# Logits made for four chunks at once, pairs for two chunks, and two score products moved, in a DeltaNet and expert kernel

## The chip, the cores and the metric

The kernel runs on one core of one Trainium2 chip. The metric is device time in microseconds. Before the change the median of 3 runs is 493.04 us (491.14 to 493.22).

## The reference, cut to what matters

Attention comes first, for 4 batches, 8 heads, 768 steps and a head size of 48. Each head of each batch keeps a 48x48 state:

```
k_n = k / (norm(k) + 1e-6)
for t in range(768):
    y[t]  = q[t] @ state
    v_old = k_n[t] @ state
    state = state + beta[t] * outer(k_n[t], v[t] - v_old)
```

The outputs y of all heads, side by side, are the tokens x: 3072 rows of 384. A gate then sends every token to one of 16 experts: 4 group logits `x @ w_group`, the best group, 4 expert logits `x @ w_expert[g]`, the best expert in it, and a weight that is the product of the two softmax values. The result of a token is that weight times `relu(x @ w1) @ w2` of its expert (384 to 1024 to 384). All is float32.

## The kernel before, in words

**Stages.** The 768 steps are cut into 24 chunks of 32 (`C`, `NCH`); one chunk of all 4 batches fills 128 partitions. Chunks go in groups of four (`RG`). A first stage runs attention and gate chunk by chunk, and a second stage runs the 16 experts. In the listing PE is TensorE, DVE VectorE, ACT ScalarE, POOL GpSimd and SP the engine that issues loads. A float32 matmul of the program appears in the trace as two instructions.

**Order of work.** Within the first stage the order on every engine is the order in which the code is written, and each engine takes its list in that order. The DVE list is partly made by small tasks: `inverse(g)` and `route(r)` are generators that `work(n)` advances by a budget, and `allow(...)` lets a task pass a named point.

**Scores.** `gram(u)` (L242) makes the products k k and k q of chunk u: 32 matmuls (64 instructions in the trace) into one PSUM buffer, copied by ACT into `gt` (L262, for the inverse) and `gq` (L268, for the output). It is called for chunks 0 to 7 in the opening (`first_grams`, the k k part of chunks 0 to 3 first and their k q part last), for chunks 8 and 9 just after, and then for chunk u+10 in period u (`ahead_of`). The opening uses three PSUM places in turn (`homes`); later all of `g_ps`, `t_ps` and `l_ps` share the one buffer with the tag "g".

**Inverse.** `inverse(g)` (L289) turns the scores of four chunks over on DVE (L297), takes roots, solves 32x32 triangular systems by DVE products and sums (L367, L373), and turns the result back (L401, `mt`). ACT spreads it into `mtb` (L412), DVE for a few parts (L410). For group 0 the square root is ACT's, and an Exp behind it (L322) loads the table that the gate needs later. For later groups POOL computes the roots.

**A period.** `advance(u)` (L461) has four steps: the state times k (L471), copied to `f`, and the state times q (L480); `w` = inverse times `f` (L488); the state's sum `s_ps` (L499), copied to `s_bd` by two ACT operations (L505); and the output (L513, or L518 for chunks 14 to 19), copied to `x` by ACT (L522) and stored. `mask(u)` and `scale(u)` (L448, it makes `vh` from `kv`) are DVE work for coming chunks, and `put_values` (L458) copies `vh` into PSUM on ACT. `vh` has two buffers.

**Gate.** `logits(u)` (L533) turns the 128 rows of x by three TensorE transposes (L540), copies them (`xt`, L546), multiplies them with `wr` (384x20) by L441, and copies the 20 logits to `lg` (L552). It belongs to chunk u-1 in period u. `route(r)` works on the logits of four chunks: it is started in the period two behind the group's last chunk, finds expert, rank and weight, and ends in sorting products into PSUM (L706), one per period, which period 22 completes and reads.

**Loads.** `begin(...)` ties a load to a moment: ACT writes one column of the tile (L784), which holds the load on SP until ACT has come there. `con` holds constants in two parts; the second holds the identity. Just before the first period the kernel multiplies constants into the state's PSUM place (L817, two matmuls of 128x384), whose result is overwritten later.

Of the kernel before, what the change touches and what calls it, by code (L numbers as in the profile page):

```python
# [16 lines left out]
C = 32  # L17
# [49 lines left out]
def deltanet_then_moe(  # L67
# [27 lines left out]
    BL, DB = 32, DM // 4  # L95
    assert len(SLOTS) == NE == 16 and not any(n <= TILE or n > T * TILE for n in SLOTS)
# [16 lines left out]
    wr = cp.tile([128, DC, NL], F32, name="wr")  # L113
# [63 lines left out]
    with ExitStack() as first:  # L177
# [14 lines left out]
        ENDING = NCH - 2  # L192
        halved = range(LATE, SMALL * RG)
# [46 lines left out]
        def gram(u, home=None, parts=(0, 1)):  # L240
# [47 lines left out]
        def inverse(g):  # L288
# [243 lines left out]

        def logits(u):  # L533

            r = group_of[u]
            if u == groups[r][0]:
                lg_[r] = sm.tile([128, RG, NL], F32, tag="lg", name=f"lg{r}", bufs=3)
            t_ps = ps.tile([128, DC, 128], F32, tag="g", name=f"t_ps{u}")
# [6 lines left out]
            xt = wk.tile([128, DC, 128], F32, tag="xt", name=f"xt{u}")  # L545
            nc.scalar.activation(xt, t_ps, ACT.Copy)  # L546
            yield
            l_ps = ps.tile([128, NL], F32, tag="g", name=f"l_ps{u}")
            for j in range(DC):
                (in_quarters if u >= ENDING else at_once)(l_ps, xt[:, j], wr[:, j], j == 0,  # L550
                                                          j == DC - 1)
            nc.scalar.activation(lg_[r][:, u - groups[r][0]], l_ps, ACT.Copy)  # L552
# [224 lines left out]
        with tc.manual_schedule(engines={mybir.EngineType.PE, mybir.EngineType.DVE,  # L777
# [28 lines left out]
            ahead = advance(0)  # L806
            next(ahead)
# [8 lines left out]
            for n in (H * D, H * D):  # L816
                nc.tensor.matmul(s_ps[:, 0, 0:n], lhsT=ident, rhs=con[:, cols[1]:cols[1] + n],  # L817
                                 start=True, stop=True, skip_group_check=True)
            second = inverse(1)
# [10 lines left out]
            ahead_of = {u: [u + LEAD] if u + LEAD < NCH else [] for u in range(NCH + 1)}  # L830
            begun, x_in = set(), {}
# [45 lines left out]
            for u in range(NCH + 1):  # L877
# [23 lines left out]
                if not later:  # L901
                    next(turned)
# [24 lines left out]
                for v in ahead_of[u]:  # L927
                    gram(v)
                if ahead_of[u] or later or ending:
# [12 lines left out]
                next(step)  # L942
                if u < NCH - 1:
# [385 lines left out]
```

## Time and profile before

| | |
|---|---|
| median of 3 runs | 493.04 us |
| profiled execution, its own time | 492.32 us |
| its span | 490.6 us |
| PE busy in the span | 447.1 us (91%) |
| DVE busy | 236.1 us (48%) |
| ACT busy | 193.8 us (40%) |
| POOL busy | 188.9 us (39%) |

The profile is of one execution. Busy shares are means over stages that differ, so the windows of the next section but one divide the span. The first stage ends near 218 us. In the timeline a row is one instruction or a series of like ones: start, duration, engine, line, operation, output and input, count, and in brackets the idle time of the engine before it with what ended it; "issue" means that no wait of the profile explains it. The granted clock is the share of TensorE's full speed (2.4 GHz) that was granted, 0.50 being 1.2 GHz.

### The profile page before, as it was taken

To read this page: it belongs to the slowest core of one execution; us is meant where nothing else is said; L and a number is where in the kernel's file an instruction comes from. 1 tells how busy PE (TensorE), PEld (TensorE's weight loads), DVE (VectorE), ACT (ScalarE), POOL (GpSimd) and SP (SyncE) were. 2 spreads that over 40 slices of the span, in tenths; PEclk is the share of its full clock that TensorE was granted. 3 is DMA by queue.
4 is the path that set the end of the run, shared out by engine and by line. 5 is a ranking of instruction groups with operands and counts; after the bars stand their busy time and mean duration, and the time that the engine had idled before them with its cause. 6 is when DMAs were issued, how large, how long until landed. Compare 5 with 4: busy or idle time off the path is not lost. (4 is left out here: it accounts for less than half of the span.)

```text
span 490.6 us, 18139 instructions
## 1 busy us (share of the span) xinstructions
PE 447.1 (91%) x7738; PEld 422.6 (86%) x7738; DVE 236.1 (48%) x866; ACT 193.8 (40%) x415; POOL 188.9 (39%) x328
## 2 busy tenths in 40 slices
PE   3437999999999999999999999999999999999992
PEld 3325888888888888889999999999999999999992
DVE  2998999999999994465201201220122012201210
ACT  3416978798887766641112112111211111111110
POOL 0041210634517132102466355544645465265122
PEclk9999999999999989999999999999999999999998
DMA  5466454454356533106978877967977797878830
GB/s 165 141 193 190 154 168 146 131 173 149 93 165 179 180 106 106 59 22 171 364 227 252 277 255 204 310 181 246 339 260 234 270 330 276 253 221 305 278 112 31
DMA packets 56741, 97.07 MB, mean 198 GB/s; under 512 B 18958, under 2 KB 41417, under 8 KB 56659
## 3 DMA queue, kind: packets, MB, share of 16 engines
q1 hardware_dynamic: 50739, 85.89, 54.7%
q0 software_dynamic: 5920, 10.00, 6.7%
q8 instruction: 62, 1.02, 0.9%
q14 instruction: 20, 0.16, 0.1%
HBM read 81.75 MB, written 14.27 MB: 196 GB/s over the span
## 5 line engine op out<-in xcount | busy, mean ns | idle before, releaser
L1113 PE MATMUL y_ps<-hid,w 128*128 128x224 f32 (+15 forms) x768 | 132.2, 331 | 0.0
L1113 PEld LDWEIGHTS y_ps<-hid,w 128*128 128x128 f32 x768 | 129.0, 190 | 0.3
L1094 PE MATMUL h_ps<-xt,w 128*128 128x232 f32 (+14 forms) x720 | 122.7, 330 | 0.0
L1094 PEld LDWEIGHTS h_ps<-xt,w 128*128 128x128 f32 x720 | 120.1, 190 | 0.3
L1066 POOL DMA_INDIRECT xq<-x_dram,from_q x92 | 87.6, 953 | 37.0 <-issue 24.6
L1097 ACT ACTIVATE hid<-h_ps 128x448 f32<-128x448 f32 (+15 forms) x64 | 32.1, 502 | 100.2 <-PE h_ps L1094 100.2
L1116 DVE COPY yt<-y_ps 128x232 f32<-128x232 f32 (+13 forms) x14 | 5.1, 366 | 135.3 <-PE y_ps L1113 135.3
L1125 POOL DMA_INDIRECT out_dram<-yo,to_i x32 | 34.0, 1064 | 91.3 <-DVE yo L1163 80.3
L1118 ACT ACTIVATE yt<-y_ps 128x224 f32<-128x224 f32 (+15 forms) x34 | 11.5, 337 | 116.6 <-PE y_ps L1113 116.6
L373 DVE TENSOR_TENSOR m<-m,below 128x16 f32<-128x16 f32 (+4 forms) x180 | 53.8, 299 | 0.3
L367 DVE TENSOR_TENSOR below<-m 128x16 f32<-128x16 f32 (+4 forms) x180 | 52.5, 293 | 0.1
L505 ACT ACTIVATE s_bd<-s_ps 48x768 f32<-48x768 f32 x46 | 37.0, 805 | 6.0 <-PE s_ps L499 5.1
L1163 DVE TENSOR_SCALAR yo<-yr,gate 128x384 f32<-128x384 f32 (+14 forms) x28 | 11.1, 415 | 48.5 <-DMA yr<-y_dram 39.8
L257 PE MATMUL g_ps<-kqt 48*32 48x64 f32 (+1 forms) x1216 | 19.4, 236 | 15.3 <-issue 7.9
L257 PEld LDWEIGHTS g_ps<-kqt 48*32 48x32 f32 x1216 | 14.8, 116 | 17.8 <-issue 12.9
L488 PEld LDWEIGHTS w_ps<-f,mtb 64*64 64x64 f32 x736 | 23.7, 137 | 5.6 <-ACT f L475 3.8
L412 ACT ACTIVATE mtb<-mt,con 128x256 f32<-128x256 f32 x39 | 28.2, 747 | 0.0
L488 PE MATMUL w_ps<-f,mtb 64*64 64x48 f32 x736 | 26.6, 222 | 1.5 <-ACT f L475 1.4
L499 PE MATMUL s_ps<-w,kv 32*112 32x96 f32 x736 | 24.5, 267 | 1.2 <-issue 0.5
L499 PEld LDWEIGHTS s_ps<-w,kv 32*112 32x112 f32 x736 | 20.5, 172 | 3.8 <-ACT w L492 0.8
L471 PE MATMUL a_ps<-s_bd,kqt 112*32 112x96 f32 x736 | 21.2, 253 | 2.3 <-ACT s_bd L505 1.3
L592 POOL TENSOR_TENSOR acc<-acc,hots 128x16 f32<-128x16 f32 x16 | 4.2, 261 | 47.1 <-DVE hots L590 46.1
(176 smaller groups left out, 577.2 us busy)
## 6 DMA issues: line engine op xcount, KB each, us to landing
w<-in_w_dram SPq DMA_DIRECT2D x29, 1536.0 KB, 8.8
kv<-in_kv_dram SPq DMA_DIRECT2D x24, 416.0 KB, 3.6
kqt<-in_kq_dram SPq DMA_DIRECT2D x20, 448.0 KB, 4.1
x_dram<-x SPq DMA_DIRECT2D x24, 192.0 KB, 2.3
w<-in_w_dram SPq DMA_DIRECT2D x24, 128.0 KB, 3.9
y_dram<-yq SPq DMA_DIRECT2D x36, 84.0 KB, 9.0
yr<-y_dram SPq DMA_DIRECT2D x14, 192.0 KB, 2.4
kqt<-in_kq_dram SPq DMA_DIRECT2D x8, 224.0 KB, 3.9
```

The lines of the kernel that those rows point to most:

```text
L257: nc.tensor.matmul(g_out[quads[b], hh * NP + j, of], lhsT=kqt[rows, 0, j, quads[b]], rhs=kqt[rows, of, j, quads[b]], start=True, stop=True ...
L367: nc.vector.tensor_tensor(t, column.to_broadcast(like), row.to_broadcast(like), op=ALU.mult)
L373: nc.vector.tensor_tensor(to, to, t, op=ALU.add)
L412: nc.scalar.activation(mtb[:, rows, a], from_, ACT.Copy, scale=by)
L488: nc.tensor.matmul(w_ps[b, h], lhsT=mt[b, uu * H + (h % 2) * NP + h // 2], rhs=f[b, h], start=(h == 0), stop=True, skip_group_check=True)
L499: nc.tensor.matmul(s_at[0:KR, b, j], lhsT=k[quads[b], j, 0:KR], rhs=w[quads[b], 2 * j:2 * j + 2], start=(u == 0 and j == 0), stop=True, sk ...
L505: nc.scalar.activation(s_bd[rows, :, :, hh, :], s_at[rows, :, :, hh * D:(hh + 1) * D], ACT.Copy)
L1066: nc.gpsimd.indirect_dma_start(out=xq[:, g, :], out_offset=None, in_=x_dram[:, :].rearrange("n (q c) -> (n q) c", q=4), in_offset=bass.Ind ...
L1094: nc.tensor.matmul(h_ps[:, k], lhsT=w1[:, j, (f + k) * 128:(f + k + 1) * 128], rhs=xt[:, j, 0:R], start=(j == 0), stop=(j == DC - 1), skip ...
L1097: nc.scalar.activation(hid[:, f:f + 2], h_ps, ACT.Relu)
L1113: nc.tensor.matmul(y_ps, lhsT=w2[:, f, j * 128:(j + 1) * 128], rhs=hid[:, f], start=(f == 0), stop=(f == FC - 1))
L1125: put = nc.gpsimd.indirect_dma_start(out=out[:, :], out_offset=bass.IndirectOffsetOnAxis(ap=to[0:P, i:i + 1], axis=0), in_=yo[0:P, :], in_ ...
```

## The change

It has five parts. Nothing else of the program differs.

1. **Pairs for chunks 0 and 1.** The first two score products are made with 64-column weights (two batches together): 16 matmuls instead of 32. ACT copies the even half with a parity factor, and one DVE operation adds the odd half. The Exp that loads the table moves from behind the square root to behind the last score product of the opening.
2. **Scores of chunks 8 and 9** move from ahead of w into period 0; chunks 10 and 11 are both made in period 1. The second one of a period comes behind the output product. The loads that hung on them are begun behind the first spread of inverse 0.
3. **Constants ahead of w.** The matmuls of constants are seven instead of two.
4. **Logits of chunks 0 to 15.** In period u the three transposes of chunk u-1 go into one tile for four chunks (for u below 14 at the end of the period). In periods 5, 9, 13 and 17 `logits_of` makes the logits of four chunks: `wr`, padded to 32 columns, is the weight, the tokens of a chunk are the moving operand, and each chunk has one strip of 32 columns of the array. The result is copied, turned back together with the next chunk's transposes, and copied to `lg`. Chunks 16 to 23 keep their own logits.
5. **Routes** of the first four groups start one period later.

```diff
@@ gram @@
+            if paired:
+                for j in range(NP):
+                    for b in pairs:
+                        for hh in range(2):
+                            k = kqt[hh * 64:hh * 64 + D, 0, j, b]
+                            nc.tensor.matmul(g_out[b, hh * NP + j], lhsT=k, rhs=k, start=True,
+                                             stop=True, skip_group_check=True)
+                even, odd = cut["parity"][:, 0:1], cut["parity"][:, 1:2]
+                part = wk.tile([128, H, C], F32, tag="part", name=f"part{u}")
+                nc.scalar.activation(part, g_out[:, :, 0], ACT.Copy, scale=even)
+                nc.vector.scalar_tensor_tensor(
+                    gts[g][:, :, uu].rearrange("p t h -> p h t"), in0=g_out[:, :, 1], scalar=odd,
+                    in1=part, op0=ALU.mult, op1=ALU.add)
+                return
@@ inverse @@
-                nc.scalar.activation(rooted, cut["tiny"], ACT.Exp)
@@ logits @@
+        def turn_x(u):
+            g, uu = divmod(u, RG)
+            if uu == 0:
+                xts_of[g] = wk.tile([128, RG, DC, 128], F32, tag="xt", name=f"xt{g}", bufs=1)
+            n = DC + len(turned_logits)
+            t_ps = ps.tile([128, n, 128], F32, tag="g", name=f"t_ps{u}")
+            for j in range(DC):
+                nc.tensor.transpose(out=t_ps[:, j], in_=xs[u][:, j * 128:(j + 1) * 128],
+                                    identity=ident)
+            if turned_logits:
+                logits_by_token(t_ps[:, DC])
...
+            nc.scalar.activation(xts_of[g][:, uu], t_ps[:, 0:DC], ACT.Copy)
+        def logits_by_token(t_ps=None):
...
+            nc.tensor.transpose(out=t_ps, in_=l_sb, identity=ident)
+            lg_[r] = sm.tile([128, RG, NL], F32, tag="lg", name=f"lg{r}", bufs=3)
+            nc.scalar.activation(lg_[r], t_ps.rearrange("p (u e) -> p u e", e=BL)[:, :, 0:NL],
+                                 ACT.Copy)
+        def logits_of(r):
+            l_ps = ps.tile([128, 128], F32, tag="g", name=f"l_ps{r}")
+            for j in range(DC):
+                for uu in range(RG):
+                    nc.tensor.matmul(l_ps[quads[uu]], lhsT=wr[:, j], rhs=xts_of[r][:, uu, j],
+                                     start=(j == 0), stop=(j == DC - 1), skip_group_check=True)
+            l_sb = wk.tile([128, 128], F32, tag="l_sb", name=f"l_sb{r}", bufs=1)
+            nc.scalar.activation(l_sb, l_ps, ACT.Copy)
@@ opening @@
-                gram(u, homes[i % len(homes)], parts)
+                gram(u, homes[i % len(homes)], parts, i < 2)
...
+            nc.scalar.activation(rooted, cut["tiny"], ACT.Exp)
...
-            for u in range(2 * RG, LEAD):
-                gram(u, homes[u % len(homes)])
-                begin(after_gram[u])
...
-            for n in (H * D, H * D):
+            for n in [H * D] * 7:
...
                 allow(ACT_STEP)
+            for u in range(2 * RG, LEAD):
+                begin(after_gram[u])
@@ periods @@
+            ahead_of.update({u: [2 * RG + 2 * u, 2 * RG + 2 * u + 1] for u in range(2)})
...
-                r = group_of.get(u - 2)
-                if r is not None and group_of.get(u - 1) != r and r < NGR - 2:
+                r = group_of.get(u - 3)
+                if r is not None and group_of.get(u - 2) != r and r < NGR - 2:
                     start(route(r), 0.25)
+                if 1 < u < LOGITS + 2 and u % RG == 1:
+                    logits_of((u - 2) // RG)
...
-                for v in ahead_of[u]:
+                for v in ahead_of[u][:1]:
                     gram(v)
...
                 next(step)
+                for v in ahead_of[u][1:]:
+                    gram(v)
+                if early:
+                    next(turned)
```

Here `LOGITS` is 16 and `early` is u below 14.

## Rows read from the trace of the kernel before

**Rows 1.** Busy time by stage: the stretch in us, its length, busy us of each engine with its instructions, granted clock, DMA share, GB/s.

```profile
43.00:146.00 103.00, 96.57 (x3259) 85.29 (x3254) 101.83 (x424) 86.69 (x171) 33.77 (x102) 1.00 0.48 147
146.00:188.00 42.00, 39.13 (x1240) 34.83 (x1238) 39.58 (x152) 30.66 (x62) 19.65 (x51) 0.96 0.52 157
188.00:218.00 30.00, 29.23 (x698) 26.28 (x694) 13.88 (x68) 17.89 (x40) 2.15 (x2) 1.00 0.18 56
218.00:484.00 266.00, 263.67 (x1634) 262.03 (x1632) 49.55 (x104) 44.54 (x101) 125.17 (x141) 1.00 0.77 248
```

**Rows 2.** What DVE waited for between 10 and 180 us: us in total, times, longest.

```profile
DVE m L297 <- ACT gt L262: 8.0, 1, 8.0
DVE vh L448 <- PE w_ps L488: 1.9, 1, 1.9
```

**Rows 3.** Timelines of DVE, ACT and PE around the hand-over of the inverses of chunks 16 and 20.

```profile
152.25 1.18 DVE L401 STREAM_TRANSPOSE mt<-m 128x1024 f32<-128x1024 f32 x1
...
178.56 1.25 DVE L401 STREAM_TRANSPOSE mt<-m 128x1024 f32<-128x1024 f32 x1
...
157.31 1.43 ACT L412 ACTIVATE mtb<-mt,con 128x256 f32<-128x256 f32 x2
...
159.17 1.13 PE L488 MATMUL w_ps<-f,mtb 64*64 64x48 f32 x32 [0.65 <-ACT f L475]
...
187.51 1.14 PE L488 MATMUL w_ps<-f,mtb 64*64 64x48 f32 x32
```

**Rows 4.** Timeline of all engines, the opening.

```profile
6.84 0.53 PE L257 MATMUL g_ps<-kqt 48*32 48x32 f32 x31
...
9.22 0.49 PE L257 MATMUL g_ps<-kqt 48*32 48x32 f32 x33 [1.84 <-issue]
9.82 0.60 ACT L262 ACTIVATE gt<-g_ps 128x256 f32<-128x256 f32 x1 [2.13 <-PE g_ps L257]
10.45 1.25 DVE L297 STREAM_TRANSPOSE m<-gt 128x1024 f32<-128x1024 f32 x1 [7.96 <-ACT gt L262]
...
12.10 1.28 ACT L322 ACT_TABLE_LOAD   x1
```

**Rows 5.** Timeline of all engines from the second part of the constants to the second group's turn (the last row from the DVE timeline further on).

```profile
30.74 0.22 POOL L803 COPY what<-con 128x48 f32<-128x48 f32 x1 [15.30 <-DMA con<-in_const_dram]
...
34.12 0.66 PE L257 MATMUL begin<-kqt 48*32 48x32 f32 x37 [5.27 <-issue]
...
35.73 1.25 DVE L401 STREAM_TRANSPOSE mt<-m 128x1024 f32<-128x1024 f32 x1
...
37.88 0.38 SPq L203 DMA_DIRECT2D kv<-in_kv_dram  x1
...
38.34 0.88 PE L257 MATMUL g_ps<-kqt 48*32 48x64 f32 x38 [1.52 <-issue]
...
39.16 2.93 PE L817 MATMUL s_ps<-con 128*128 128x384 f32 x4
...
42.01 1.17 PE L488 MATMUL w_ps<-vh,mtb 64*64 64x48 f32 x32
...
43.23 0.56 DVE L448 TENSOR_TENSOR vh<-kv,normt 128x384 f32<-128x384 f32 x1 [1.86 <-PE w_ps L488]
...
55.94 1.24 DVE L297 STREAM_TRANSPOSE m<-gt 128x1024 f32<-128x1024 f32 x1
```

**Rows 6.** Timeline of PE from w(2) to w(3), one period with a gram.

```profile
56.82 1.13 PE L488 MATMUL w_ps<-f,mtb 64*64 64x48 f32 x32
57.88 0.86 PE L257 MATMUL g_ps<-kqt 48*32 48x64 f32 x64
58.67 1.04 PE L499 MATMUL s_ps<-w,kv 32*112 32x96 f32 x32
59.84 0.84 PE L441 MATMUL l_ps<-wr,xt 128*128 128x20 f32 x6
60.62 1.13 PE L513 MATMUL o_ps<-w,gqm 64*64 64x48 f32 x32
61.68 0.87 PE L471 MATMUL a_ps<-s_bd,kqt 112*32 112x96 f32 x32
...
63.14 0.55 PE L540 MATMUL t_ps<-con,x 128*128 128x128 f32 x3
63.62 1.14 PE L488 MATMUL w_ps<-f,mtb 64*64 64x48 f32 x32
```

**Rows 7.** The page's list of loads: count, KB each, median us from issue to landing.

```profile
kv<-in_kv_dram SPq DMA_DIRECT2D x24, 416.0 KB, 3.6
```

**Rows 8.** Timeline of PE, the state products that open periods 15, 16 and 19.

```profile
150.82 0.87 PE L471 MATMUL a_ps<-s_bd,kqt 112*32 112x96 f32 x32
...
156.88 0.90 PE L471 MATMUL a_ps<-s_bd,kqt 112*32 112x96 f32 x29 [0.15 <-ACT s_bd L505]
...
178.42 1.34 PE L471 MATMUL a_ps<-s_bd,kqt 112*32 112x96 f32 x32
```

**Rows 9.** PE by the microsecond around the half clock: stretch, length, busy, granted clock, DMA share, GB/s.

```profile
179.00:180.00 1.00, 1.00 (x33) 0.50 0.56 200
```

**Rows 10.** What PE waited for between 42 and 216 us: us in total, times, longest.

```profile
PE g_ps L257 <- issue: 2.5, 4, 0.8
```

More of the change, by code (lines that the diff above doesn't have):

```diff
@@ L95, in deltanet_then_moe @@
     BL, DB = 32, DM // 4
+    assert NL <= BL
     assert len(SLOTS) == NE == 16 and not any(n <= TILE or n > T * TILE for n in SLOTS)
@@ L112, in deltanet_then_moe @@
     ident, before, ones = cut["ident"], cut["before"], cut["ones"]
-    wr = cp.tile([128, DC, NL], F32, name="wr")
+    wr = cp.tile([128, DC, BL], F32, name="wr")
     acc = cp.tile([128, NCH + 1, NE], F32, name="acc")
@@ L192, in deltanet_then_moe @@
         ENDING = NCH - 2
+        LOGITS = NCH - 2 * RG
         halved = range(LATE, SMALL * RG)
@@ L238, in deltanet_then_moe, with gram @@
         begun_with = {}
-        def gram(u, home=None, parts=(0, 1)):
+        def gram(u, home=None, parts=(0, 1), paired=False):
             g, uu = divmod(u, RG)
@@ L531, in deltanet_then_moe @@
         sorted_in = {}
[L533 to L538, printed above, removed]
+        xts_of, turned_logits = {}, {}
+        def turn_x(u):
[4 more added lines that the diff above has]
+            t_ps = ps.tile([128, n, 128], F32, tag="g", name=f"t_ps{u}")
             for j in range(DC):
@@ L544, in logits @@
             xs.pop(u)
-            xt = wk.tile([128, DC, 128], F32, tag="xt", name=f"xt{u}")
-            nc.scalar.activation(xt, t_ps, ACT.Copy)
-            yield
[L548 to L552, printed above, removed]
+            nc.scalar.activation(xts_of[g][:, uu], t_ps[:, 0:DC], ACT.Copy)
+        def logits_by_token(t_ps=None):
+            (r, l_sb), = turned_logits.items()
+            turned_logits.clear()
+            if t_ps is None:
+                t_ps = ps.tile([128, 128], F32, tag="g", name=f"lt_ps{r}")
+            nc.tensor.transpose(out=t_ps, in_=l_sb, identity=ident)
[10 more added lines that the diff above has]
+            nc.scalar.activation(l_sb, l_ps, ACT.Copy)
+            turned_logits[r] = l_sb
+        def logits(u):
+            r = group_of[u]
+            if u >= LOGITS and u == groups[r][0]:
+                lg_[r] = sm.tile([128, RG, NL], F32, tag="lg", name=f"lg{r}", bufs=3)
+            turn_x(u)
+            yield
+            if u >= LOGITS:
+                xt = xts_of[u // RG][:, u % RG]
+                l_ps = ps.tile([128, NL], F32, tag="g", name=f"l_ps{u}")
+                for j in range(DC):
+                    (in_quarters if u >= ENDING else at_once)(l_ps, xt[:, j], wr[:, j, 0:NL], j == 0,
+                                                              j == DC - 1)
+                nc.scalar.activation(lg_[r][:, u - groups[r][0]], l_ps, ACT.Copy)
             yield
@@ L805, in deltanet_then_moe @@
                                   .to_broadcast([128, 4, 4, BL]))
-            ahead = advance(0)
-            next(ahead)
-            for u in range(2 * RG, LEAD):
-                gram(u, homes[u % len(homes)])
-                begin(after_gram[u])
             begin_with.close()
@@ L815, in deltanet_then_moe @@
             sorted_in.update(at=s_ps[:, 0, H * D:H * D + T * 3 * NE], begun=True)
-            for n in (H * D, H * D):
+            for n in [H * D] * 7:
                 nc.tensor.matmul(s_ps[:, 0, 0:n], lhsT=ident, rhs=con[:, cols[1]:cols[1] + n],
                                  start=True, stop=True, skip_group_check=True)
+            ahead = advance(0)
+            next(ahead)
             second = inverse(1)
@@ L900, in deltanet_then_moe @@
                 later, ending = LATE <= u < NCH - 2, u + 2 == NCH
-                if not later:
+                early = u < LATE
+                if not later and not early:
                     next(turned)
@@ L926, in deltanet_then_moe @@
                     gathered = gather_first(found_0)
-                for v in ahead_of[u]:
+                for v in ahead_of[u][:1]:
                     gram(v)
-                if ahead_of[u] or later or ending:
+                if early:
+                    next(step)
+                elif ahead_of[u] or later or ending:
                     next(step)
@@ L942, in deltanet_then_moe @@
                 next(step)
+                for v in ahead_of[u][1:]:
+                    gram(v)
+                if early:
+                    next(turned)
                 if u < NCH - 1:
@@ L1311 @@
         beta=bt.reshape(128, NCH // RG * C), const=const,
-        wr=wr.reshape(DM // 128, 128, G + G * Eg).transpose(1, 0, 2),
+        wr=np.pad(wr, [(0, 0), (0, 32 - wr.shape[1])]).reshape(DM // 128, 128, 32).transpose(1, 0, 2),
         w1=w1.reshape(G * Eg, 4, DM // 128, 32, F).transpose(0, 2, 1, 3, 4).reshape(G * Eg, DM, F),
```

## The prediction

> **What bounds the kernel now.** I read the stages first [rows 1]: from 43 to 146 us PE is busy 96.57 of 103 us and DVE 101.83, ACT only 86.69; from 188 on DVE has slack; from 218 to 484 PE is busy 263.67 of 266. So the expert stage is a PE-bound block that only moves with the end of the first stage, and the change touches the first stage alone. There two engines are full, and the reader has to see which one sets the pace. By its waits DVE waits only twice for more than half a microsecond between 10 and 180 us, 8.0 us at its start and 1.9 us once [rows 2]: it works through its fixed list at its own speed. PE does too. Who is ahead is told by the hand-over every four chunks (w(u) is the first TensorE product with the inverse of chunk u, L488): for chunk 16 DVE ends the inverse at 152.25 + 1.18 = 153.43, ACT takes it at 157.31, w(16) starts at 159.17; for chunk 20 DVE ends at 179.81 and w(20) starts at 187.51 [rows 3]. So now PE, with ACT between its steps, sets the time, and DVE comes next with 157.31 - 153.43 = 3.9 us in hand at chunk 16. What PE saves beyond those 3.9 us plus what DVE itself gains is not paid out.
>
> **The start of DVE's list.** Its first transpose runs at 10.45, behind ACT's copy of chunk 3's scores at 9.82, behind matmuls that stop after 31 of 64 and go on at 9.22 with a hole of 1.84 that no wait explains [rows 4]. Such holes come after matmul 223, 350, 477, 604, 731 and 858 of the program, 127 apart (the first is the 64 + 128 + 31 of [rows 4], the last stands before the 38.34 row [rows 5]; six in all): the instruction stream arrives in blocks. Pairs for chunks 0 and 1 take 2 x 32 matmuls out, so chunk 3 ends at matmul 192, inside the block. Its matmuls then end near 7.5 instead of 9.7 (they start about 0.3 earlier, and 33 of them take 0.49), the copy of 0.60 near 8.3. Lead 2.1 us; bounds 0 (something else of chunk 3 is late) and 2.3. The two added DVE operations (128x256) cost 0.2 to 0.6 us each, below the vh row of 0.56 for 128x384 [rows 5], inside the 7.96 us in which DVE idles: nothing. The page Runtime: NRT & Kernel Launch of the Trainium skill (Instruction fetch mechanics) says that crossing a block boundary is mostly hidden. The holes of 1.84 and 5.27 us [rows 4, 5] say otherwise here; by the page this term would be nothing, and 486.6 below would be 488.7.
>
> **Where w(0) starts.** Now at 42.01, behind two fillers (39.16, 2.93 us for 4 instructions), behind the scores of chunks 8 and 9, behind two holes of 5.27 and 1.52 us [rows 5]. After: 704 matmuls of scores instead of 896 stand before the fillers, so matmul 731 falls inside w(0) and the hole of 5.27 no longer stands in front. The fillers read constants that land at 30.74 (the POOL row) or, since the earlier bursts of loads shift by about a microsecond, near 29.5. Fourteen instructions follow: at the 0.7 us that four now take on average, 9.8 us; if they run at twice the speed from about the middle on, 7.4. End between 36 and 39.3; I take 36.9. The inverse is ready at 35.73 + 1.25 - 2.1 and one spread of 0.7, so 35.6: PE is last here. Lead of w(0): 5.1 us, bounds 2.7 and 6. The table load (1.28 us [rows 4]) that moves behind the scores lies where ACT waited for PE in the hole of 5.27; without that cover it costs 1.5 us, still under the fillers.
>
> **Periods 0 and 1.** Each gets one more gram, 0.80 us by the distance of 57.88 to 58.67 [rows 6]. In period 1 the turn of x now stands behind the second gram in the one shared PSUM buffer and waits for two ACT copies (0.60 for the first [rows 4]), about 1.0 us. The first logits (0.78, 59.84 to 60.62) go. w(0) to w(2), 14.8 us before [rows 5, 6], becomes 16.5. Lead of PE at w(2): 3.4, bounds 1.0 and 4.3. DVE wants the copy of chunk 11's scores at 55.94 [rows 5] less its lead; it comes near 50.6: no stall, and 1 us of one if w(0) comes 3 us later.
>
> **DVE's second lead.** Its wait of 1.86 at 43.23 is for w(0) [rows 5] and goes. Next late is that operation's own data: the load of kv 2 was issued at 37.88 and now stands on SP behind a load that ACT releases only after the first spread, about 36.2; kv loads land 3.6 us after issue in the median [rows 7], so near 40.6 with another load ahead. DVE's lead becomes 43.23 - 40.6 = 2.6 us; bounds 1.5 and 4.0 (2.1 + 1.9).
>
> **Periods 2 to 13.** Per chunk, six matmuls of 128x128 by 20 columns go (0.78 us). Per four chunks come 24 of 128x32 by 128 columns and one transpose. The trace has no such form. Nearest is L471, 112x32 by 96 columns: 32 instructions are busy for 0.87 us [rows 6], 0.027 each, times 128/96: 24 take 0.87. Upper end: the four column strips don't overlap, 24 x 0.13 as for L441's six: 3.1. I take 0.87, for L471 works on the same strips. The transpose is 0.16 (63.14 to 63.62 for three). So (4 x 0.78 - 0.87 - 0.16) / 4 = 0.5 us a period, at the upper end -0.04. A period without a gram takes 6.06 (150.82 to 156.88 [rows 8]), held by the round through ACT, and the gram's matmuls stand where PE waits for ACT in that round, so against 6.80 (56.82 to 63.62 [rows 6]) there is room for the 0.5. Twelve periods give 6.0 us; PE alone would lead by 9.4 at w(14). The page TensorEngine Tiling (Array Packing) of the Trainium skill (Tiling Modes, Key Properties) says that tiles work in parallel, but that a change of the tiling mode drains the array. L471's 0.027 us agrees with the parallel part; the new group follows matmuls of the same strip form, so by the page it drains once behind itself, which no row here prices.
>
> **Where it is capped.** At w(16) DVE allows 2.6 + 3.9 = 6.5 us. PE's 9.4 is above it, so PE waits some 3 us for DVE around chunks 12 to 16 and 6.5 are left. Between 14 and 19 the round of 6.06 holds, so nothing is saved; period 17 pays for its 24 logit matmuls ahead of w, 0.6. The routes start a period later, so one more sorting pair is left over in period 22, 0.2. At w(20) DVE allows 2.6 + 187.51 - 179.81, over 10, and doesn't bind. Sum: 6.5 - 0.6 - 0.2 = 5.7 us off the profiled execution's 492.32 (span 490.6 and 1.7 around it): 486.6; off the median of 493.04, 0.7 above that execution: 487.3. I say 487.0.
>
> **The rivals.** (1) More: DVE keeps the full lead of 4.0, and the stretch at half clock (0.50 at 179 us [rows 9]) isn't met again before the tail: 4.0 + 3.9 - 0.8 + 1.0, about 8, 484.5. For it: both of DVE's waits have named causes that go; against: kv 2. Chance 0.13. (2) Less: DVE's lead is at its lower bound (1.5 + 3.9 - 0.8 = 4.6), or the strips don't overlap and PE keeps the lead of w(2) alone (3.4 - 0.5 - 0.8 = 2.1): 488 to 490.5, say 489. For it: the missing form; against: L471. Chance 0.19. (3) No change: the instruction stream is the pace. A faster PE uses up its blocks faster, and what it saves comes back as holes, as the 5.27 and 1.52 now do; w(0) leads by 2.7, w(2) by 1.0, and the 0.8 at the end eats it: 492.5. For it: matmul 731 now lies inside w(0); against: 2.5 us of such holes ahead of grams in all from 42 to 216 [rows 10]. Chance 0.10. (4) Slower: the clock. PE, now the engine that waits, falls to half speed again and again; about 179 to 182 one such stretch made a state product 1.34 us [rows 8] instead of 0.87, and three groups of that size together lose about 1.5. From period 14 on a round has no slack, so four such stretches there or in the tail outweigh 5.7 us, and seven give 492.5 + 5 = 497. For it: PE will idle in about a tenth of each period; against: a granted clock of 1.00 from 43 to 146 and 0.96 to 188, one fall in all [rows 1]. Chance 0.08.
>
> **How the numbers follow.** Forecast 0.50 (484.8 to 488.8), rivals as above. About 0.5%, 2.5 us, is what can be told from no change: 490.6 and 495.5 are the lines. Faster: 0.50 + 0.13 + most of rival 2 (0.15) = 0.78; same 0.04 + 0.09 = 0.13; slower 0.09. The range leaves out the better half of rival 1, rival 4 and most of rival 3: 483.8 to 491.2.
>
> **What would show it.** Right: the first DVE transpose near 8.3; fillers from about 29.5 and w(0) near 37; no DVE wait above 1 us behind it; 24 strip matmuls in under 1 us; ACT's spreads for chunk 16 waiting for DVE, and w(20) near 181.6. Wrong: w(0) after 40, a DVE wait above 2 us for the scores of chunk 11 or for kv 2, logit groups of 2 to 3 us, or a granted clock of 0.50 in several stretches after 45 us.

## The result, and the profile after

The changed kernel takes 497.38 us in the median (493.56 to 500.26, 20 runs), the kernel before 493.13 (489.06 to 503.41, 20 runs). The ratio, which leaves out executions more than 1.5% above the fastest of their kernel, is 1.0097, with a 95% interval of 1.0072 to 1.0122: slower by 1%, where 487.0 and "faster" had been forecast. The profiled execution took 499.14 us (span 496.9; before 492.32 and 490.6).

By stage, the columns being those of [rows 1], with the borders behind 146 moved to the changed kernel's times:

```profile
43.00:146.00 103.00, 91.10 (x3151) 79.56 (x3128) 98.17 (x407) 80.53 (x156) 34.74 (x95) 0.92 0.46 143
146.00:192.00 46.00, 40.37 (x1380) 35.77 (x1380) 43.30 (x168) 35.25 (x70) 19.33 (x53) 1.00 0.50 156
192.00:226.00 34.00, 32.60 (x731) 28.96 (x724) 15.35 (x72) 17.43 (x40) 5.75 (x7) 0.90 0.16 49
226.00:490.00 264.00, 262.07 (x1566) 260.68 (x1565) 48.30 (x99) 43.86 (x99) 125.17 (x140) 1.00 0.78 250
```

The expert stage is what it was: 262 of 264 us of PE. The first stage now runs at a granted clock of 0.92 and 0.90 in two of its three stretches. PE alone, in finer stretches (length, busy, granted clock, DMA share, GB/s):

```profile
38.00:44.00 6.00, 5.00 (x244) 1.00 0.88 253
44.00:48.00 4.00, 0.71 (x31) 1.00 0.81 227
49.00:61.00 12.00, 11.10 (x288) 0.50 0.30 96
62.00:95.00 33.00, 29.26 (x1093) 1.00 0.52 155
96.00:99.00 3.00, 3.00 (x63) 0.50 0.21 71
100.00:208.00 108.00, 98.79 (x3303) 1.00 0.44 137
209.00:215.00 6.00, 6.00 (x110) 0.50 0.34 93
```

Three stretches at the lower level (1.2 GHz) instead of the one of [rows 9], and ahead of the first one PE does almost nothing for four microseconds. The opening, from the timeline of all engines (to be compared with [rows 4, 5]):

```profile
7.75 0.88 PE L273 MATMUL g_ps<-kqt 48*32 48x32 f32 x64
...
9.30 1.25 DVE L313 STREAM_TRANSPOSE m<-gt 128x1024 f32<-128x1024 f32 x1 [1.35 <-ACT gt L278]
...
31.23 6.33 PE L863 MATMUL s_ps<-con 128*128 128x384 f32 x14 [2.17 <-DMA con<-in_const_dram]
...
37.66 1.14 PE L503 MATMUL w_ps<-vh,mtb 64*64 64x48 f32 x32
...
38.13 0.38 SPq L205 DMA_DIRECT2D kv<-in_kv_dram  x1
38.60 0.85 SPq L201 DMA_DIRECT2D kqt<-in_kq_dram  x2
...
42.02 0.79 PE L528 MATMUL o_ps<-w,gqm 64*64 64x48 f32 x21 [1.00 <-issue]
...
44.72 0.56 DVE L463 TENSOR_TENSOR vh<-kv,normt 128x384 f32<-128x384 f32 x1 [3.28 <-DMA kv<-in_kv_dram]
...
48.87 1.18 PE L495 MATMUL o_ps<-s_bd,kqt 112*32 112x96 f32 x21 [4.16 <-issue]
```

w(0) starts at 37.66, 4.35 us earlier than before, as forecast. Then DVE waits 3.28 us for kv 2, and PE stops in the middle of a group of 32 (11 before, 21 after) for 4.16 us with no wait that the profile shows. The DMA view of those microseconds, 40.5 to 46 and 46 to 47, tells what is missing (packets, MB, share of 16 engines):

```profile
q1 hardware_dynamic: 480, 1.60, 102.3%
...
q1 hardware_dynamic: 145, 0.25, 84.5%
q8 instruction: 1, 0.02, 7.1%
```

For 5.5 us the queues carry loads and not one packet of instructions; the one that comes after 46 is followed by PE at 48.87. How long a packet can take to come is told by two blocks: the kernel before began one at 34.12 [rows 5], and the next packet ran before 36, with load packets at 15% and less; the changed kernel began one at 42.02, and the next packet ran after 46, with load packets at 86% and more. Later the trace has nine such packets in the 40 us from 60 to 100. How far the changed kernel is behind (w(u) after minus before, us; the last row is the changed kernel's second profile, from run e17_again):

| | w(0) | w(1) | w(2) | w(3) | w(13) | w(18) | w(22) | w(23) | span |
|---|---|---|---|---|---|---|---|---|---|
| profile | -4.35 | +0.26 | +5.19 | +4.56 | +4.02 | +3.82 | +2.24 | +6.04 | +6.3 |
| second profile | -3.33 | -0.82 | +4.32 | +7.19 | +4.24 | +3.58 | +1.58 | +2.74 | +3.6 |

The loss is made between w(0) and w(2), 24.35 us where 14.81 were before, and partly won back; the end differs from one execution to the next.

### The profile page after: what moved, and what is told of

The parts are those of the page before. It is cut to its first block, busy times and chain, and to the rows that moved or that the text cites. A ratio compares the mean times of both kernels' runs of the same rounds, so it can differ in the third digit from the quotient of the medians.

```text
span 496.9 us, 18024 instructions
## 1 busy us (share of the span) xinstructions
PE 448.8 (90%) x7688; PEld 422.6 (85%) x7688; DVE 237.9 (48%) x868; ACT 193.1 (39%) x407; POOL 193.4 (39%) x328
## 4 chain that ended last, share of the span: by engine, by line
PE 61%; issue 12%; DMA 9%; ACT 9%; POOL 4%; SPq 1%; DVE 1%; POOLq 0%; DVEq 0%
PE y_ps L1173 19%; PE h_ps L1154 19%; PE w_ps L503 4%; PE s_ps L514 3%; DMA y_dram<-yq 3%; PE a_ps L486 3%; DMA kqt<-in_kq_dram 3%; ACT s_bd L520 3%; PE o_ps L495 3%; DMA yr<-y_dram 2%; PE o_ps L528 2%; PE g_ps L273 2%; ACT mtb L427 2%; POOL out_dram L1185 1%; PE t_ps L558 1%
## 5 line engine op out<-in xcount | busy, mean ns | idle before, releaser
L388 DVE TENSOR_TENSOR m<-m,below 128x16 f32<-128x16 f32 (+4 forms) x180 | 51.9, 288 | 0.4
L1223 DVE TENSOR_SCALAR yo<-yr,gate 128x384 f32<-128x384 f32 (+14 forms) x28 | 11.2, 415 | 44.6 <-DMA yr<-y_dram 36.9
L318 POOL MEMSET m<- 128x256 f32 (+4 forms) x30 | 4.2, 191 | 59.1 <-DVE m L313 59.1
L514 PE MATMUL s_ps<-w,kv 32*112 32x96 f32 x736 | 25.6, 273 | 1.4 <-issue 1.1
L528 PE MATMUL o_ps<-w,gqm 64*64 64x48 f32 x576 | 23.0, 230 | 3.9 <-issue 3.8
L495 PE MATMUL o_ps<-s_bd,kqt 112*32 112x96 f32 x736 | 22.3, 264 | 4.2 <-issue 4.2
L528 PEld LDWEIGHTS o_ps<-w,gqm 64*64 64x64 f32 x576 | 20.3, 144 | 5.9 <-issue 4.3
```

The lines of the kernel that those rows point to most:

```text
L388: nc.vector.tensor_tensor(to, to, t, op=ALU.add)
L495: nc.tensor.matmul(o_ps[quads[b], 2 * j:2 * j + 2, :], lhsT=kqt[0:KR, 1, j, quads[b]], rhs=s_bd[0:KR, b, j], start=(j == 0), stop=False, s ...
L514: nc.tensor.matmul(s_at[0:KR, b, j], lhsT=k[quads[b], j, 0:KR], rhs=w[quads[b], 2 * j:2 * j + 2], start=(u == 0 and j == 0), stop=True, sk ...
L528: nc.tensor.matmul(o_ps[b, h], lhsT=gq[b, hq].rearrange("p a t -> p (a t)"), rhs=w[b, h], start=(u == 0 and h == 0), stop=True, skip_group ...
```

## The experiments

Ratios are to the kernel before on the same chip, with 95% intervals. "Theory 1" is that the four loads begun together behind the first spread hold up kv 2 and PE's instructions.

**The opening alone, and its loads moved.** The opening (e5_head) is the diff without `turn_x`, `logits_of`, `logits_by_token` and without the later start of the routes. The loads (e1_loads) are the whole change with

```diff
             nc.scalar.activation(rooted, cut["tiny"], ACT.Exp)
+            for u in range(2 * RG, LEAD):
+                begin(after_gram[u])
             allow(BEGUN)
...
-            for u in range(2 * RG, LEAD):
-                begin(after_gram[u])
             mask(0)
```

> The kernel before with the opening of the change alone: paired grams of chunks 0 and 1, the Exp behind the grams, scores of chunks 8 to 11 in periods 0 and 1, seven fillers, the loads behind the first spread. Logits and routing stay as in the kernel before. Theory 1 (the four loads hold back kv 2 and the next block of TensorE's instructions): a hole of 3 to 5 us in period 0 or 1, half clock behind it, w(2) at 60 to 62 us and nothing won back later, time 495 to 498 us. Rival (the opening's loss in the changed kernel came from the new logits): w(2) at or before 54 us, time 489 to 491 us.

> The four loads behind the first spread (kqt 10, kv 2, kqt 11 and 12) are begun ahead of the fillers instead, right behind the moved Exp; nothing else changes. Theory 1 (the burst of loads holds back kv 2 and a block of TensorE's instructions, TensorE stands still for 4.16 us in period 1 and its clock halves): no hole of over 2 us in periods 0 and 1, VectorE waits under 1 us for kv 2, the clock is full at w(2), w(2) at about 56 us instead of 62.01, time 488 to 492 us. Rival 1 (TensorE outruns its instructions wherever the loads are): the hole of about 4 us stays, the clock halves behind it, time 496 to 499 us.

Measured: 1.0084 (1.0053 to 1.0114) and 1.0010 (0.9978 to 1.0042). PE with the opening alone, its timeline and then its stretches:

```profile
42.39 0.49 PE L493 MATMUL o_ps<-s_bd,kqt 112*32 112x96 f32 x11
47.31 0.87 PE L493 MATMUL o_ps<-s_bd,kqt 112*32 112x96 f32 x21 [4.43 <-issue]
...
61.52 1.13 PE L501 MATMUL w_ps<-f,mtb 64*64 64x48 f32 x32
```

```profile
44.00:47.00 3.00, 0.00 (x0) 1.00 0.55 170
48.00:61.00 13.00, 13.00 (x303) 0.50 0.28 88
```

The old logits and the same hole at the same place, the same 13 us at half clock, w(2) at 61.52: the opening makes the loss by itself. With the loads earlier (w(0) at 36.99):

```profile
39.81 0.54 PE L528 MATMUL o_ps<-w,gqm 64*64 64x48 f32 x11
43.93 1.31 PE L528 MATMUL o_ps<-w,gqm 64*64 64x48 f32 x21 [3.58 <-issue]
...
57.30 1.14 PE L503 MATMUL w_ps<-f,mtb 64*64 64x48 f32 x32
```

DVE's wait for kv 2 is gone (that `vh` runs at 40.38, unwaited), the half clock behind the hole lasts some 7 us instead of 13.65, and w(2) is at 57.30: 4.7 us come from where the loads stand, and the ratio, 1.0010 against 1.0097, is no longer apart from 1. A second half clock, from 138 to 149, follows a wait of 1.96 us for POOL, of which more below. But the hole stays, 3.58 us, one block earlier; theory 1 as I had put it said that it would go. The packet of instructions again comes only after 41, with load packets at 91% of the queues from 37.5 to 41.

**Loads spread.** Does the hole follow the loads? e9_stagger is e1_loads with kqt 11 and 12 begun only behind the first store of x (its edit, shortened, follows); e19_spread and e20_spread2 were to spread the loads further, on top of mends told below:

```diff
-        after_gram = {2 * RG: [of_kq(2 * RG + 2), (kv_[2], [lambda: load_kv(2)])],
-                      2 * RG + 1: [of_kq(2 * RG + 3), of_kq(NB)]}
+        after_gram = {2 * RG: [(kv_[2], [lambda: load_kv(2)]), of_kq(2 * RG + 2)],
+                      2 * RG + 1: []}
...
+                if u == 0:
+                    load_kq(2 * RG + 3)
+                    load_kq(NB)
```

> The run with the early loads once more, with kv 2 and kqt 10 ahead of the fillers, and kqt 11 and 12 begun only at the end of period 0, so that about 0.9 MB less stands in the queues when period 0 needs its next block of instructions. Theory 1 in its narrower form (the block of instructions stands behind bulk loads in the DMA queues): its packet runs by about 39 us instead of 41.5, the hole in period 0 falls from 3.58 to under 1.5 us, no half clock before 60 us, w(2) at 53 to 55 us instead of 57.30. Rival 1 (a block takes its 6 us from request to use whatever the loads do): the hole stays over 3 us. Time 488 to 491 us by the first, 491 to 493 us by the rival.

> The same spread loads in the version with all four groups' logits at once (sorting of groups 0 to 2 a period later, of group 3 a period earlier than the change has it). The same expectations for periods 0 to 2; ratio 0.985 to 0.994 if the spread takes the hole away, 0.995 to 1.001 if it doesn't.

Measured: 1.0028 (0.9986 to 1.0069) for e9_stagger, 0.9998 (0.9965 to 1.0031) for e20_spread2, 1.0051 (1.0011 to 1.0090) for e19_spread, whose expectation was the same one with a range of 0.985 to 0.995. In e20_spread2 the two loads of kqt 11 and 12 still went out together, at 44.86. PE there, then its stretches:

```profile
44.71 1.31 PE L495 MATMUL o_ps<-s_bd,kqt 112*32 112x96 f32 x32
46.90 1.13 PE L503 MATMUL w_ps<-f,mtb 64*64 64x48 f32 x32 [0.87 <-ACT f L490]
...
50.81 1.30 PE L514 MATMUL s_ps<-w,kv 32*112 32x96 f32 x22 [1.44 <-issue]
...
59.56 1.89 PE L503 MATMUL w_ps<-f,mtb 64*64 64x48 f32 x32
```

```profile
52.00:61.00 9.00, 8.10 (x193) 0.50 0.38 124
```

No hole in period 0, where the queues are empty from 40 to 42; and one in period 1, after 402 load packets and no packet of instructions from 43 to 47.6. In e9_stagger the larger hole likewise moved, from 40.35 to 47.66 (3.20 us; 1.42 were left at 43.14). So the long holes stand where loads run beside the next block. That they would vanish without loads is not shown: no run had an opening without a burst somewhere, and the hole of 1.52 us in the kernel before [rows 5] came with the queues empty from 36 to 37.9. That TensorE outruns its instructions, the rival, is thus true as well, for holes of this size; the loads make them longer. And the clock fell for 9 us behind a wait of 0.87 and a hole of 1.44, so a hole made smaller won nothing here.

**Paired grams and Exp alone** (e12_pairs).

> The kernel before with the paired grams of chunks 0 and 1 and the Exp behind the grams alone. The profile of the changed kernel had the first transpose 1.15 us earlier by them. If that lead reaches the end of the opening: w(0) at about 41 us, ratio 0.997 to 0.999. Rival (the lead is lost in the wait for the constants, for kv 0 and for instructions, as mt(0) of the changed kernel came only 0.18 us earlier): w(0) within 0.3 us of 42.01, ratio 0.999 to 1.002.

Measured 1.0018 (0.9974 to 1.0062): no difference in time. Inside, its profile (of an execution of 498.55 us; the median is 495.83) shows neither of the two expected cases:

```profile
38.04 1.33 PE L501 MATMUL w_ps<-vh,mtb 64*64 64x48 f32 x32
...
43.64 0.55 PE L526 MATMUL o_ps<-w,gqm 64*64 64x48 f32 x12 [1.80 <-issue]
```

w(0) is 3.97 us earlier by the pairs alone, with the scores of chunks 8 and 9 still ahead of it; then come a hole of 1.80 us, half clock from 45 to 58, and w(2) at 58.17, later than before. So in this execution an early w(0) was followed by a hole and a half clock even without the seven matmuls of constants and with the scores and loads in their old order.

**The routing a period later.** e4_logits is the kernel before with the new logits and their routing; e11_late has the old logits and only

```diff
-                r = group_of.get(u - 2)
-                if r is not None and group_of.get(u - 1) != r and r < NGR - 2:
+                r = group_of.get(u - 3)
+                if r is not None and group_of.get(u - 2) != r and r < NGR - 2:
```

> The kernel before with the logits of four chunks at once and the routing of them alone (the opening, the seven fillers and the scores of chunks 8 and 9 stay as before). Theory 1 (the opening loses 5 us, the logits gain): w(2) within 0.5 us of 56.82, each of periods 2 to 13 shorter by 0.3 to 0.5 us, time 489 to 492 us with the tail's loss in it. Rival (the logits themselves are given back to the clock or to the instruction stream): time 493 to 496 us.

> The kernel before with one thing changed: the routing of groups 0 to 3 is started one period later. Logits, opening and everything else stay. Theory 4 (this delay alone puts GpSimd's table behind the place of its use in TensorE's order): a wait of 1 to 4 us for GpSimd in one of periods 8 to 13, half clock behind it, and 14 sorting matmuls in period 22 with w(23) 2 to 4 us later against w(22); time 1.007 to 1.015 of the kernel before. Rival (the delay hurts only because the new logits make TensorE's period shorter than VectorE's and GpSimd's part of it): no wait of over 0.5 us, ratio 0.997 to 1.004.

Measured: 1.0076 (1.0040 to 1.0112) and 1.0064 (1.0024 to 1.0103). In e4_logits w(2) is at 55.15, and PE later waits 4.08 us for POOL, with 10 us of half clock behind it. e11_late, PE, then POOL, then DVE, then PE by stretches:

```profile
105.84 0.55 PE L540 MATMUL t_ps<-con,x 128*128 128x128 f32 x3
109.11 0.46 PE L706 MATMUL s_ps<-mine,at 128*128 128x96 f32 x2 [2.72 <-POOL at L624]
...
99.77 0.21 POOL L640 TENSOR_TENSOR cw<-sums,cw 128x4 f32<-128x4 f32 x1
104.30 3.05 POOL L678 TENSOR_TENSOR what<-what,half 128x24 f32<-128x24 f32 x1 [4.32 <-DVE what L674]
...
103.11 0.20 DVE L664 TENSOR_REDUCE place<-rk 128x4 f32<-128x64 f32 x1
```

```profile
43.00:111.00 68.00, 61.62 (x2140) 1.00 0.46 150
112.00:121.00 9.00, 9.00 (x149) 0.50 0.29 91
122.00:226.00 104.00, 97.56 (x2919) 1.00 0.36 114
```

A period later, DVE has the products of the next inverse in its list ahead of `place`: POOL's `cw` is done by 99.98 and waits 4.32 us for DVE. POOL's product of 24 elements a row then takes 3.05 us; in the kernel before the same one took 0.23, at 98.06. PE's order hasn't moved its first sorting matmul to match, so PE stands 2.72 us, and its clock is at half for some 10 us. The Trainium skill's page SBUF — State Buffer (Terms) says that DVE and POOL share one pair of ports, and that the one that comes second waits for the other's whole instruction; one such wait would be 0.54 us at most here, the longest DVE instruction beside it, so it doesn't explain the 3.05 us by itself. In the kernel before DVE was at work as well, and no run here settles what held POOL.

Two ways out: allow the sorting of groups 0 to 2 a period later (e7_sort: one more `yield NEXT` ahead of the first SORT), or start the routes at the end of the period that turns the logits back (e8_start).

> The logits part alone (as in the run of that part), with the sorting matmuls of groups 0 to 2 allowed one period later, so that TensorE doesn't stand before them for GpSimd's table. Theory 4 (the routing begun a period later puts GpSimd's table behind the place that TensorE's order gives its use; TensorE waits up to 4.08 us there, and its clock halves for 10 us): no wait for GpSimd in periods 8 to 20, no half clock between 100 and 125 us, w(10) at 111 to 113 us instead of 120.17, time 490 to 492 us, and an end no better than before. Rival (the clock falls in those periods because TensorE has less to do): a half clock of like length at another place in periods 4 to 14, time 494 to 497 us.

> The logits part alone, with the routing of a group started at the end of the period in which its logits are turned back (half a period earlier than the change has it, half a period later than the kernel before). Theory 4: GpSimd's first table is ready before TensorE's order comes to it, or the wait is under 1 us; no half clock behind it; the sorting of period 22 falls back to about 12 matmuls as before, time 488 to 491 us. Rival (it isn't the start of the routing): a wait of over 2 us for GpSimd or a half clock of 7 to 10 us stays, time 494 to 497 us.

Measured: 0.9984 (0.9942 to 1.0026) and 1.0126 (1.0079 to 1.0173). With the later sorting, what PE waited for from 42 to 216 us has no wait for POOL over 0.9:

```profile
PE a_ps L487 <- ACT s_bd L521: 4.1, 12, 0.7
...
PE s_ps L457 <- POOL acc L643: 0.9, 1, 0.9
```

and w(10) is at 113.94 (115.57 before). Starting earlier also brought the sorting forward; PE then waited 3.17 us for the same table, until 99.95, and the clock was at half from 101 to 110. What counts here is the order between PE's place for the sorting and DVE's and POOL's list, not the date of the start.

**The end of the pipeline.** In the first profile period 22 holds 14 sorting matmuls (12 before), a half clock follows, and w(23) comes 11.53 us behind w(22) (7.73 before). e2_route and e18_route2, the same kernel twice, give group 3 its old logits and start; e17_again is the changed kernel unchanged:

```diff
-        LOGITS = NCH - 2 * RG
+        LOGITS = NCH - 3 * RG
```

> Chunks 12 to 15 make their logits alone again, and the routing of their group starts in the period in which the kernel before starts it; groups 0 to 2 stay as in the changed kernel. Theory 3 (the late routing puts 14 sorting steps and a wait for GpSimd into period 22, and the clock falls behind it): no half clock between periods 20 and 23, w(23) some 3 to 4 us earlier against w(22) than in the changed kernel, time about 493.5 us. Rival (the clock falls there anyway, or the tail is hidden): time within 1 us of the changed kernel's, 496.5 to 498.5 us.

> The changed kernel once more, unchanged, on the chip of the runs beside it. If the loss belongs to the kernel and not to the chip that it ran on: ratio 1.006 to 1.013, a hole of 3 us and more in period 0 or 1 with half clock behind it, 14 sorting matmuls in period 22. Otherwise (a single chip's or execution's accident): ratio under 1.004.

> The changed kernel with group 3 as in the kernel before, once more, beside the changed kernel on one chip. If the 14 sorting matmuls of period 22 cost what the trace shows (w(23) 3.8 us later against w(22)): ratio 0.006 to 0.008 under that of the changed kernel beside it. If its first run was right (1.020) and the edit itself loses: 0.005 to 0.012 over it. If the two only differ by the clock's chance: within 0.004.

Measured: 1.0200 (1.0151 to 1.0249), then side by side on one chip 1.0097 (1.0059 to 1.0135) for the changed kernel and 1.0117 (1.0069 to 1.0165) for this one. (Why the first of the two measurements of one kernel lies 0.8% above the second isn't known.) That the changed kernel is about 1% slower came out again.

Mending the tail won no time, but the traces of all runs show that there is a loss in it. Between w(22) and w(23), the kernel before, then the changed kernel's second profile:

```profile
201.73 1.58 PE L706 MATMUL s_ps<-mine,at 128*128 128x96 f32 x12
...
203.31 1.13 PE L756 MATMUL s_ps<-mine,at 128*128 128x96 f32 x8
205.15 0.91 PE L756 MATMUL s_ps<-mine,at 128*128 128x96 f32 x6 [0.70 <-POOL at L674]
```

The ten traces with 12 sorting matmuls have w(23) 7.73 us behind w(22), or 9.15 where PE had another wait; of the ten with 14, all with the wait of 0.70 for POOL, six have 8.89 or 10.31, 1.16 more. e11_late, which starts the routes later and does nothing else, is one of the six. In the other four (11.53 to 11.99 us, the changed kernel's first profile among them) the clock was at half there too; in none of the ten with 12. So 1.16 us belong to the 14 matmuls that the later start brings, and 2.6 to 3.1 more to the clock in some executions.

Why did e18_route2 not gain the 1.16? Its edit adds a wait of its own. It puts the turn and the logits of chunk 12 right behind each other at the end of period 13, and PE waits there for ACT's copy:

```profile
147.27 0.27 PE L573 MATMUL t_ps<-con,l_sb 128*128 128x128 f32 x1
148.25 0.84 PE L456 MATMUL l_ps<-wr,xt 128*128 128x20 f32 x6 [0.71 <-ACT xt L565]
```

With this wait and the old logits of four chunks, w(13) to w(22) takes 61.61 us where e17_again takes 59.37: 2.24 lost for 1.16 won. In e2_route half clock from 148 to 155 followed the same wait. The test is thus no evidence against theory 3.

**All mends together.** e10_shift: the logits part alone with the later sorting and group 3's a period earlier. e14_all: the whole change with that and the early loads. e15_tail: the early loads, sorting of groups 0 and 1 later, group 3 as before. e16_noopen: e15_tail without the change's opening.

> The logits part alone with the sorting of groups 0 to 2 one period later (as in the run of that) and the sorting of group 3 one period earlier than the change has it, so that period 22 isn't left with 14 sorting matmuls. Theory 4: no wait of over 1 us for GpSimd, at most about 12 sorting matmuls in period 22, w(23) under 9 us behind w(22), ratio 0.991 to 0.996 of the kernel before. Rival (what the logits save comes back as half clock elsewhere): ratio 0.997 to 1.003 with 6 us or more of half clock between 40 and 220 us.

> The whole change with the loads ahead of the fillers and the shifted sorting of the two runs before. If the losses are the burst of loads and the place of the sorting: the hole in period 0 stays at 2 to 4 us with 3 to 7 us of half clock (as in the run with the early loads), no wait of over 1 us for GpSimd, ratio 0.992 to 0.998 of the kernel before. If the logits' gain is given back to the clock whatever the order: ratio 0.999 to 1.005.

> The whole change, mended in three places: the loads ahead of the fillers, the sorting of groups 0 and 1 one period later, and group 3 (chunks 12 to 15) with logits and routing as in the kernel before. If the three places are where the change lost its time: no wait of over 1 us for GpSimd, about 12 sorting matmuls in period 22, w(23) 7 to 8 us behind w(22), ratio 0.986 to 0.994 of the kernel before. If what is saved comes back as half clock elsewhere: w(22) earlier than 198 us and yet a ratio of 0.997 or more in the mean of the runs, or new stretches of half clock of 6 us and more.

> The same without the change's opening (grams, Exp, fillers and loads as in the kernel before), so logits of chunks 0 to 11 for four at once, sorting of groups 0 and 1 a period later, group 3 as before. Logits alone are worth what w(18) in the run with the shifted sorting showed, 2 to 4 us, if nothing is lost at the end: ratio 0.992 to 0.996. Rival (given back to the clock): 0.998 to 1.003.

Measured: 1.0022 (0.9986 to 1.0057), 0.9967 (0.9929 to 1.0006), 0.9997 (0.9961 to 1.0033) and 1.0003 (0.9964 to 1.0043); the early loads with group 3 as before and no later sorting (e3_both, for which 484 to 488 us was expected) gave 1.0059 (1.0019 to 1.0100). The profile of e15_tail is the fastest, PE by stretches:

```profile
37.00:100.00 63.00, 53.09 (x1986) 1.00 0.48 150
100.00:200.00 100.00, 94.26 (x3046) 1.00 0.43 137
200.00:480.00 280.00, 277.82 (x1946) 1.00 0.74 238
```

Full clock throughout, w(22) 3.36 us earlier than before, a span of 488.0 instead of 490.6. Yet its fastest run took 488.28 us and the fastest of the kernel before beside it 488.25. The mends take the change's loss away; no version is shown to be faster than the kernel before.

Where the gain goes is seen in the profiles (after minus before, us):

| | w(2) | w(13) | w(22) | w(23) | span |
|---|---|---|---|---|---|
| e14_all | -1.07 | -5.04 | -6.39 | -2.21 | +1.1 |
| e10_shift | -1.96 | -3.51 | -4.39 | -0.26 | +3.5 |
| e15_tail | -0.60 | -3.24 | -3.36 | -3.37 | -2.6 |

With all four groups' logits at once the first stage does lead by 6.39 us at w(22). The sorting of group 3 moved a period earlier didn't help: both runs still have 14 matmuls and the wait for POOL there, with half clock behind, and lose 4.1 to 4.2 us up to w(23). Another 3.3 and 3.8 us go behind w(23); why is not known. (From w(23) to the end the traces of all runs differ between 282.1 and 286.3 us.) e8_start has the new logits of all four groups with 12 matmuls in period 22, but waits for POOL of 3.17 and 2.55 us elsewhere; no run had the one without the other.

## Why the prediction was wrong

**The start of DVE's list**: first transpose forecast at 8.3, at 9.30, within the bounds. The hole of 1.84 us went with the smaller number of matmuls. The lead was lost again on the way: DVE waited 0.84 us for kv 0 at 28.71, and `mt` of group 0 came at 35.55 instead of 35.73 [rows 5].

**Where w(0) starts**: forecast 36.9, bounds 36 to 39.3, measured 37.66. Right in time, in part by luck: the matmuls of constants began at 31.23 instead of 29.5 and took 6.33 us instead of 7.4. And e12_pairs reaches 38.04 without them, so most of the lead came with the pairs. Nothing was earned by it.

**Periods 0 and 1**: this step failed. It put 16.5 us from w(0) to w(2), a lead of 3.4 with bounds of 1.0 to 4.3; measured were 24.35 and -5.19. The step counted grams and copies (its terms add up to 16.6), and no hole and no clock. I had written that the hole of 5.27 us "no longer stands in front" because matmul 731 falls inside w(0). That much came true, PE passes matmul 731 without a hole; but the holes of the next two block ends were left at nothing: 1.00 us behind matmul 857 and 4.16 behind 985. Before, group 0's inverse was being made until 36.98 [rows 5], which covered a part of the holes; w(0) early means that the same stream is used up sooner, with loads beside it and no wait to cover a hole. These two periods took 7.85 us more than forecast: the two holes, and then work at half clock, groups of 32 at 1.82 to 1.95 us where [rows 6] has 1.04 and 1.13.

**DVE's second lead**: this step failed too. kv 2 was to land near 40.6, from the median landing of [rows 7]; it was issued at 38.13, and `vh` got it at 44.72, 6.6 us later, with three kqt loads beside it. The median over 24 loads was the wrong row for one in a burst of four. At chunk 16 DVE ended the inverse at 157.14, 3.71 us later than before, where 2.6 earlier had been forecast.

**Periods 2 to 13**: the mechanism was right. 24 strip matmuls take 0.84 us (0.87 forecast), the turn back 0.27 (0.16):

```profile
112.81 0.84 PE L583 MATMUL l_ps<-xt,wr 128*32 128x128 f32 x24
...
118.65 0.27 PE L573 MATMUL t_ps<-con,l_sb 128*128 128x128 f32 x1
```

The size was off. From w(2) to w(13) e14_all gained 4.0 us, e15_tail 2.6 and e10_shift 1.6, so 0.36, 0.24 and 0.14 a period where I had 0.5; the changed kernel, with 3 us at half clock at 96, 1.2 in all. With these gains smaller, the cap by DVE was never met: even in e14_all ACT's first spread for chunk 16, at 152.52, came 1.29 us behind the end of the inverse.

**The tail**: the later routes were booked at 0.2 us for one more pair. The pair is there (14 for 12), and this term was mis-sized: it costs 1.16 us, 0.70 of them a wait for POOL that I had not counted, and a half clock in four of ten traces. What I also left out of "the routes start a period later" is that DVE's and POOL's order around the sorting changes: 1.0064 when done alone. In the two profiles of the changed kernel itself PE never waits over 0.7 us for POOL; with the loads mended (e1_loads) it waits 1.96.

**The rivals.** The time of rival 4, 497, is what came, in part by its mechanism, the clock, but not at its place: I had looked for the falls from period 14 on, and the decisive one lies between w(1) and w(2) (in the second profile up to w(3)). The rival had seven short falls and no hole, so that its number fits is luck. What I held against it, one fall in the kernel before [rows 1], came from a stretch in which PE never waited over 0.8 us at a time. On one chip the mean granted clock of the executions that the ratio counts was 0.988 before (22 runs) and 0.976 after (6 runs). Over 494 us that is 5.9 us of full-speed work, against 4.7 us between the mean times (491.16 and 495.84). It is an upper end, for the groups stretch by less than the clock falls: those from 48.87 to 62.01 lost about 5.0 us by their rows where the clock fell short by 6.8. By that ratio an estimate of 4.3 us is the clock's, most of the loss; how the holes and the savings share the rest can't be told. Rival 3 had the holes of the instruction stream, but at matmul 731, and priced them at no change.

The prediction read the Trainium skill's page Runtime: NRT & Kernel Launch (Instruction fetch mechanics), by which crossing a block boundary is mostly hidden, against the holes of the kernel before. The holes of 1.1 to 4.7 us in periods 0 and 1 of the runs with this opening speak against the page for this place; the rest of the stage, where the changed kernel's profile has no hole over 1.4 us, is nearer to it.

## What to carry to other kernels

A hole in the profile that a wait covers is covered only as long as the wait stays; before work is pulled forward, look up which loads and which block of instructions come beside it at the new time. Where TensorE runs 90% busy, price a new stop of a few microseconds with the half clock behind it: here stops of 2.4 to 4.7 us in the periods were followed by 3 to 24 us at half clock. And a task moved by one period is moved past every other queue's list, so compare its place on DVE, POOL and PE one by one; two late results that nobody waited for before can become the longest wait. When an edit that takes a loss out wins nothing, read its trace for a loss that it puts in.

## What the runs showed of the hardware

Packets of instructions and bulk loads share the DMA engines: with load packets at 102% of the queues for 5.5 us no block arrived, and PE resumed 2 to 3 us after the packet that ended the gap (46.0 to 46.5, then 48.87; 41.0 to 41.5, then 43.93 in e1_loads; 44.5 to 45.0, then 47.31 in e5_head). The same delay stands in the kernel before without loads: a packet between 35.5 and 36.0, PE at 38.34. A granted clock that had fallen stayed at half while PE was 92 to 100% busy (49 to 61 us: 11.10 of 12.00; 13.00 of 13.00 with the opening alone). And the same few microseconds of holes cost differently from one execution to the next: e15_tail had holes of 2.27 and 1.14 us in periods 0 and 1 and kept the full clock, e20_spread2 stood for 0.87 and 1.44 and lost it for 9 us; behind 3.25 us the second profile of the changed kernel had half clock from 47 to 70, behind 4.16 the first one from 48 to 62. In the opening of the kernel before PE stood for 5.27 us, after 4.45 busy us of the 10 from 20 to 30, and the clock stayed at 1.00.
